# Three parts of W2 move behind transposed rows in the transfer queue

## The chip, the cores and the metric

The kernel runs on 1 core of one Trainium2 chip. The core has five engines with instruction streams of their own: TensorE (PE in the profile; its weight loads are PEld), VectorE (DVE), ScalarE (ACT), GpSimd (POOL) and SyncE (SP), which here issues every transfer. The metric is device time in microseconds (us), the median of several runs. Lower is better.

## The reference, cut to what matters

Two layers, each an attention block and an MLP with residuals, over 2048 rows of width 512. The same weights serve both layers.

```python
def _A_ref(x, wqkv, wo):                 # H = 32 heads of 16, window W = 256
    q, k, v = ...                        # from x @ wqkv
    scores = jnp.einsum("bhqd,bhkd->bhqk", q, k) * (Dh ** -0.5)
    mask = (idx[:, None] - idx[None, :] >= 0) & (idx[:, None] - idx[None, :] < W)
    p = _softmax(jnp.where(mask[None, None], scores, -1e9), axis=-1)
    return (...einsum("bhqk,bhkd->bhqd", p, v)...) @ wo

def _B_ref(x, w1, b1, w2, b2):           # F = 1792
    h = _gelu(jnp.einsum("bsd,df->bsf", x, w1) + b1)
    return jnp.einsum("bsf,fd->bsd", h, w2) + b2

x = A_x
x = x + _A_ref(_layernorm(x), A_wqkv, A_wo)
x = x + _B_ref(_layernorm(x), B_w1, B_b1, B_w2, B_b2)
x = x + _A_ref(_layernorm(x), A_wqkv, A_wo)
x = x + _B_ref(_layernorm(x), B_w1, B_b1, B_w2, B_b2)
```

## The kernel before

The 2048 rows are 16 tiles of 128 rows. Both layers run through one stream of 32 tile visits, numbered 0 to 31, in 16 blocks of two tiles. For a block, `lnq` and `kv` normalise the rows, bring them into transposed form (`xnTA`), and make Q, K and V from them; `attention` makes scores by pieces (L733), exponentials on ACT (L740), masks on DVE or POOL (L761), the product with V (PV, L783), and its normalisation; `outproj` adds the result to X (L832). Then the rows are normalised again and transposed into `xnTB` for the MLP. The MLP works in jobs; job 0 is tiles 0 and 1, job 1 tiles 2 and 3. It multiplies by W1 in 14 chunks of 128 columns, applies GELU (some after a bias addition on DVE, L855; the others on ACT directly, L863), and then for each tile sums the 14 chunks times W2 into one bank (L632, `gT` and `W2_sb`; W1 and W2 share the name W_sb in the profile), and adds the result to X (L875).

A row is transposed by DMA: DVE writes the normalised row to a buffer `xn` (L606), and SP issues a transposing DMA from it (L611). V needs a second copy with its halves exchanged, `Vs`, which two DMAs for each tile make (L681). Weights come in by pieces, W2 in four loads (L563): chunks 0 to 3 and 4 to 7 of 512 KB each, 8 to 10 and 11 to 13 of 384 KB each.

All steps of the kernel are nodes of a plan. The order is written out by hand in the list `_ORDER`: each engine carries out its own nodes in the order of this list, so the transfers, all on SP, go out in that order too. Before a node, its engine waits for the data it reads, for the readers of what it overwrites, and, for a DMA, for the eighth DMA before it, since eight semaphores are used in turn. An SP node that waits holds up every transfer behind it. The numbers in the list that matter here:

| node | transfer | waits for |
|---|---|---|
| 50, 51, 52, 53 | W2 chunks 0-3, 4-7, 8-10, 11-13 | nothing but the eighth DMA before |
| 242, 244 | rows of tiles 0 and 1 into `xnTB`, for job 0 | `xn` from DVE |
| 526, 528 | rows of tiles 8 and 9 into `xnTA`, for block 4 | `xn` from DVE |
| 185, 186; 192, 193 | copies of V of tiles 4; 5 | V of the tile |
| 357, 358; 364, 365 | copies of V of tiles 6; 7 | V of the tile |
| 646, 648 | rows of tiles 10 and 11 into `xnTA` | `xn` from DVE |

SP's order around the edit is: V copy of tile 4 (node 185), W2 chunks 4-7, 8-10, 0-3, rows of tiles 0 and 1, V copies of tiles 5, 6, 5, rows of tiles 9 and 8, W2 chunks 11-13, V copies of tiles 4 and 7, rows of tiles 11 and 10.

Of the kernel before, what the change touches and what calls it, by code (L numbers as in the profile page):

```python
# [19 lines left out]
class _Sched:  # L20
# [154 lines left out]
    208, 170, 213, 171, 172, 43, 330, 214, 370, 206, 173, 209, 148, 371, 174, 175, 210, 149, 160, 161, 162, 372, 331,  # L175
    176, 520, 163, 215, 177, 521, 374, 164, 373, 220, 44, 211, 376, 142, 165, 221, 178, 375, 45, 166, 167, 168, 180,
    522, 169, 222, 379, 223, 181, 380, 182, 230, 523, 224, 183, 524, 231, 381, 225, 179, 226, 369, 232, 233, 184, 227,
    384, 234, 378, 185, 228, 385, 332, 229, 333, 51, 383, 342, 187, 386, 52, 334, 235, 377, 343, 335, 50, 237, 344,
    337, 394, 388, 345, 396, 382, 338, 188, 238, 236, 387, 189, 239, 190, 395, 346, 339, 240, 389, 336, 191, 398, 243,
    641, 347, 400, 348, 349, 241, 340, 350, 390, 399, 242, 352, 359, 527, 244, 402, 391, 341, 392, 351, 353, 192, 403,  # L180
    354, 306, 355, 360, 356, 361, 404, 407, 639, 357, 362, 409, 363, 193, 248, 405, 249, 262, 528, 250, 263, 408, 412,
    264, 401, 252, 393, 253, 414, 245, 246, 254, 290, 255, 247, 256, 413, 427, 257, 563, 525, 410, 259, 565, 526, 260,
    278, 261, 279, 275, 564, 640, 416, 276, 411, 428, 53, 415, 272, 422, 287, 186, 397, 281, 282, 284, 365, 288, 285,
    277, 273, 423, 406, 280, 539, 289, 540, 566, 529, 251, 530, 541, 274, 531, 542, 283, 532, 543, 307, 265, 266, 267,
    258, 269, 270, 286, 308, 533, 309, 268, 310, 311, 271, 291, 312, 313, 417, 292, 418, 293, 314, 294, 315, 419, 567,
# [761 lines left out]
```

## Time and profile before

| | |
|---|---|
| median of 3 runs | 456.76 us (456.69 to 457.06) |
| profiled execution, time | 457.15 us |
| its span, first to last instruction | 455.3 us |
| PE busy | 420.6 us (92%) |
| ACT busy | 385.0 us (85%) |
| DVE busy | 352.7 us (77%) |
| POOL busy | 193.4 us (42%) |
| transfers, the queue of all DMAs from SP | 22.17 MB, 21.0% of 16 engines |
| mean granted TensorE clock | 0.996 |

Times of single instructions are microseconds from the start of the span. The busy share of an engine is an average over the span; what an edit is worth is read from the chain that ended last, which follows the work back from the last instruction, at each step to what released it. For a DMA, SP's own duration is only the issuing; the time to landing is counted from the start of the issue to the last of its sixteen completion signals.

### The profile page before, as it was taken

Reading aid. Unit: us, or ns where it says so; the run is one execution under the profiler, and the core shown is the slowest. Engines: PE = TensorE matmul, PEld = TensorE weight load, DVE = VectorE, ACT = ScalarE, POOL = GpSimd, SP = SyncE. Lnnn points to the kernel's source line nnn. Section 1 sums busy time; section 2 is a strip of 40 time slices with the busy share of each in tenths; the row PEclk is TensorE's granted clock in tenths of the full one; section 3 lists DMA queues with packets and bytes.
Section 4 is the critical chain, followed back from the end, with each engine's and each line's share of the span. In section 5 each row is a group of like instructions: output and inputs, shape, how many; then the busy total and the mean of one; then the engine's idle time right before and its main releaser. Section 6 shows DMA issues by size and latency. Waiting matters only on the chain.

```text
span 455.3 us, 16821 instructions
## 1 busy us (share of the span) xinstructions
PE 420.6 (92%) x7506; PEld 230.2 (51%) x7579; DVE 352.7 (77%) x655; ACT 385.0 (85%) x456; POOL 193.4 (42%) x217
## 2 busy tenths in 40 slices
PE   8998999985779997899999999999999999999997
PEld 4564646543344553445455454555554454444673
DVE  5999689886775778894799867977897598756862
ACT  2997968987889899789998998999888989899633
POOL 4164634237331247632472754274243443526130
PEclk9999999999899999999999999999999999999999
DMA  8695311201400211310012021010232003002110
GB/s 243 186 218 166 77 33 24 44 10 18 86 15 1 25 23 41 76 26 1 14 35 58 1 56 37 10 42 3 62 50 62 1 4 79 14 1 67 60 48 24
DMA packets 47972, 23.25 MB, mean 51 GB/s; under 512 B 33180, under 2 KB 47900, under 8 KB 47900
## 3 DMA queue, kind: packets, MB, share of 16 engines
q1 hardware_dynamic: 47900, 22.17, 21.0%
q8 instruction: 60, 0.98, 0.9%
q14 instruction: 12, 0.10, 0.1%
HBM read 8.00 MB, written 2.10 MB: 22 GB/s over the span
## 4 chain that ended last, share of the span: by engine, by line
PE 69%; DVE 15%; ACT 12%; issue 3%; DMA 2%; POOL 0%; SPq 0%
PE ps L632 52%; ACT E L740 11%; PE ps L733 8%; PE ps L783 7%; DVE KT L666 2%; DVE E L761 2%; DVE OD L792 2%; DVE xn L606 2%; PE ps L525 1%; DVE stat L584 1%; DMA xnTB<-xn 1%; DVE OT L806 1%; DVE X L832 1%; DMA xnTA<-xn 1%; DVE X L875 1%
## 5 line engine op out<-in xcount | busy, mean ns | idle before, releaser
L740 ACT ACTIVATE E<-ps 128x1024 bf16<-128x1024 f32 x300 | 283.1, 1041 | 42.4 <-PE ps L733 41.7
L761 POOL TENSOR_TENSOR E<-E,mask 128x512 bf16<-128x512 bf16 (+2 forms) x97 | 104.2, 1089 | 88.1 <-ACT E L740 88.0
L632 PE MATMUL ps<-xnTB,W_sb 128*128 128x512 bf16 (+1 forms) x542 | 110.2, 335 | 4.2 <-issue 1.6
L632 PE MATMUL ps<-W_sb,gT 128*128 128x512 bf16 x415 | 110.1, 380 | 3.3 <-issue 2.2
L761 DVE TENSOR_TENSOR E<-E,mask 128x512 bf16<-128x512 bf16 (+2 forms) x139 | 70.1, 529 | 10.3 <-ACT E L740 10.1
L632 PE MATMUL ps<-xnTA,Wqkv_sb 128*128 128x256 bf16 x512 | 74.6, 273 | 2.1 <-ACT E L740 0.7
L632 PEld LDWEIGHTS ps<-xnTB,W_sb 128*128 128x128 bf16 x560 | 50.6, 97 | 44.7 <-issue 4.1
L733 PE MATMUL ps<-QT,KT 32*128 32x128 bf16 (+3 forms) x1920 | 60.4, 232 | 10.9 <-ACT E L740 2.9
L632 PEld LDWEIGHTS ps<-W_sb,gT 128*128 128x128 bf16 x448 | 39.6, 98 | 43.2 <-issue 3.6
L733 PEld LDWEIGHTS ps<-QT,KT 32*128 32x128 bf16 x1920 | 28.6, 93 | 62.5 <-ACT E L740 36.9
L632 PEld LDWEIGHTS ps<-xnTA,Wqkv_sb 128*128 128x128 bf16 x512 | 46.9, 98 | 25.3 <-issue 3.9
L792 DVE STREAM_TRANSPOSE OD<-ps 128x1024 f32<-128x1024 f32 x32 | 39.8, 1244 | 21.5 <-PE ps L783 21.2
L863 ACT ACTIVATE gT<-ps,b1T 128x512 bf16<-128x512 f32 (+1 forms) x80 | 43.6, 609 | 10.3 <-PE ps L632 9.9
L871 POOL TENSOR_TENSOR Xb<-X,b2all 128x512 f32<-128x512 bf16 x32 | 38.5, 1209 | 24.8 <-DVE X L875 24.8
L783 PE MATMUL ps<-E,Va 64*17 64x128 bf16 (+3 forms) x1920 | 44.0, 230 | 4.1 <-ACT E L740 1.8
L666 DVE TENSOR_TENSOR KT<-ps,parmask 128x1024 bf16<-128x1024 f32 x32 | 38.8, 1212 | 11.1 <-PE ps L632 10.8
L783 PE MATMUL ps<-E,Vs 64*17 64x128 bf16 (+3 forms) x1920 | 44.6, 230 | 0.0
L783 PEld LDWEIGHTS ps<-E,Va 64*17 64x17 bf16 x1920 | 37.4, 84 | 13.9 <-issue 8.8
L584 DVE BATCH_NORM_STATS2 stat<-X 128x6 f32<-128x512 bf16 x64 | 42.7, 677 | 1.8 <-DMA X<-in_A_x_dram 1.7
L855 DVE TENSOR_SCALAR gT<-ps,b1T 128x512 bf16<-128x512 f32 (+1 forms) x60 | 36.5, 629 | 7.0 <-PE ps L632 6.4
L800 POOL TENSOR_TENSOR Nb<-OD,Rc 128x512 bf16<-128x512 f32 x19 | 20.2, 1061 | 49.9 <-DVE Rc L796 39.6
L632 PE MATMUL ps<-Wo_sb,OT 128*128 128x512 bf16 x120 | 37.2, 388 | 3.4 <-DVE OT L806 2.5
(50 smaller groups left out, 363.0 us busy)
## 6 DMA issues: line engine op xcount, KB each, us to landing
Vs<-Va SPq DMA_DIRECT2D x64, 68.0 KB, 2.1
W_sb<-in_B_w_dram SPq DMA_DIRECT2D x4, 512.0 KB, 5.5
out_dram<-X SPq DMA_DIRECT2D x16, 128.0 KB, 1.9
X<-in_A_x_dram SPq DMA_DIRECT2D x3, 512.0 KB, 7.3
Wqkv_sb<-in_A_wqkv_dram SPq DMA_DIRECT2D x4, 256.0 KB, 5.3
W_sb<-in_B_w_dram SPq DMA_DIRECT2D x1, 768.0 KB, 6.5
W_sb<-in_B_w_dram SPq DMA_DIRECT2D x2, 384.0 KB, 4.8
Wqkv_sb<-in_A_wqkv_dram SPq DMA_DIRECT2D x1, 512.0 KB, 7.1
```

The lines of the kernel that those rows point to most:

```text
L584: add("dve", lambda e, B, t=t, k6=k6: e.bn_stats(stat6[:, k6, :], X[:, t, :]), reads=["X%d" % t], writes=["st%d" % k6], key="bs%d" % (k + j))
L632: r = e.matmul(ps[:, B[g][0], cols], lhsT, rhs, start=st, stop=sp)
L666: add("dve", lambda e, B, g=g, i=i: e.tensor_tensor(out=KT[:, kb, 2 * i : 2 * i + 2].rearrange("p c m a q -> p a (c m) q"), in0=ps[:, B[g] ...
L733: x = e.matmul(ps[:, bk[r], o : o + n], KT[rows, kb, c, m].rearrange("p a q -> p (a q)"), QT[rows, c, q : q + n], start=True, stop=True)
L740: add("act", lambda e, B, g_=g_, gi=gi: e.activation(E[:, 2 * gi : 2 * gi + 2, e0 : e0 + 512], ps[:, B[g_][0] : B[g_][0] + 2, :], AF.Exp, ...
L761: fn = lambda e, B: e.tensor_tensor(out=Ew, in0=Ew, in1=Mw, op=ALU.mult)
L783: x = e.matmul(ps[32 * r : 32 * r + VW, B[g][par], c % 2 * 2 * P + lo : c % 2 * 2 * P + hi], V[rows, (2 * b + m // 2) % VR, c * HC + 2 * r ...
L792: add("dve", lambda e, B: e.transpose(OD[:, s].rearrange("p a c q -> p (a c q)"), ps[:, B[g][0] : B[g][0] + 2, :]), reads=["ps:" + g], wri ...
L800: return e.tensor_tensor(out=Nb[:, s, :].rearrange("p (k a d) -> p a k d", a=2, d=Dh), in0=sums[:, :, :, 0:Dh], in1=rc[:, :, :, None].to_b ...
L855: add("dve", lambda e, B, g=g, fc=fc: e.tensor_scalar(out=gT[:, fc, c0 : c0 + M], in0=ps[:, B[g][0], 0:M], scalar1=b1T[:, fc : fc + 1], sc ...
L863: add("act", lambda e, B, g=g, fc=fc: e.activation(gT[:, fc, c0 : c0 + M], ps[:, B[g][0], 0:M], AF.Gelu_apprx_tanh, bias=b1T[:, fc : fc + ...
L871: add("pool", lambda e, B, t=t, xs=xs: e.tensor_tensor(out=Xb[:, xs, :], in0=X[:, t, :], in1=b2all[:], op=ALU.add), reads=["X%d" % t, "b2a ...
```

## The change

Only `_ORDER` differs. Nodes 51, 52 and 50 leave their places after the V copy of tile 4. Nodes 50 and 51 (W2 chunks 0 to 7) stand after node 244 (tile 1's row into `xnTB`); node 52 (chunks 8 to 10) stands after node 526 (tile 8's row into `xnTA`), ahead of node 53. SP's order becomes: V copy of tile 4, rows of tiles 0 and 1, W2 chunks 0-3 and 4-7, V copies of tiles 5, 6, 5, rows of tiles 9 and 8, W2 chunks 8-10, 11-13, V copies of tiles 4 and 7, rows of tiles 11 and 10. No other engine's order changes, and no instruction is added or taken away. Cut to the lines where nodes enter or leave:

```diff
-    384, 234, 378, 185, 228, 385, 332, 229, 333, 51, 383, 342, 187, 386, 52, 334, 235, 377, 343, 335, 50, 237, 344,
...
-    641, 347, 400, 348, 349, 241, 340, 350, 390, 399, 242, 352, 359, 527, 244, 402, 391, 341, 392, 351, 353, 192, 403,
...
-    264, 401, 252, 393, 253, 414, 245, 246, 254, 290, 255, 247, 256, 413, 427, 257, 563, 525, 410, 259, 565, 526, 260,
+    384, 234, 378, 185, 228, 385, 332, 229, 333, 383, 342, 187, 386, 334, 235, 377, 343, 335, 237, 344, 337, 394, 388,
...
+    348, 349, 241, 340, 350, 390, 399, 242, 352, 359, 527, 244, 50, 51, 402, 391, 341, 392, 351, 353, 192, 403, 354,
...
+    401, 252, 393, 253, 414, 245, 246, 254, 290, 255, 247, 256, 413, 427, 257, 563, 525, 410, 259, 565, 526, 52, 260,
```

## The prediction

> **What bounds the kernel now.** I read the page first. TensorE (PE) is busy for 92% of the span, and the chain that ended last lies mostly on it, so a transfer counts only where PE, or an engine that PE waits for, stands still for it.
>
> ```profile
> span 455.3 us, 16821 instructions
> ...
> PE 69%; DVE 15%; ACT 12%; issue 3%; DMA 2%; POOL 0%; SPq 0%
> ```
>
> DMA has 2% of the chain, 9 us, and the transfer queue itself (SPq) nothing. So the question is whether the moved loads touch that 2%, or get into the way of a transfer that has slack today. All that moves lies between 33 and 56 us. Next I read SP's own timeline there (start, duration, line, operation).
>
> ```profile
> 32.56 0.46 SPq L681 DMA_DIRECT2D Vs<-Va  x1
> 33.07 2.47 SPq L563 DMA_DIRECT2D W_sb<-in_B_w_dram  x3
> 39.42 2.51 SPq L611 DMA_TRANSPOSE xnTB<-xn  x2
> 41.98 2.86 SPq L681 DMA_DIRECT2D Vs<-Va  x3
> 44.88 5.25 SPq L611 DMA_TRANSPOSE xnTA<-xn  x2
> 50.18 0.59 SPq L563 DMA_DIRECT2D W_sb<-in_B_w_dram  x1
> 50.82 1.13 SPq L681 DMA_DIRECT2D Vs<-Va  x2
> ```
>
> The three W2 loads are issued from 33.07 to 35.54; then SP issues nothing until 39.42, the transpose of tile 0. What it waits for stands in SP's waits of 32 to 52 us (total, times, longest):
>
> ```profile
> SPq L127 <- DVE xn L606: 5.9, 2, 3.8
> SPq L127 <- ACT Va L575: 3.3, 1, 3.3
> SPq L127 <- DVE Va L573: 1.1, 1, 1.1
> ```
>
> The 3.8 us are the gap before tile 0's transpose: the normalised row `xn` was not ready, and it went out 0.1 us after DVE had written it (39.34). The other 2.1 us of that line are the gap before tile 8's transpose (46.77 to 48.94). The 1.1 us are the gap between tile 5's and tile 6's V copies (42.56 to 43.73). Then the chain of waits (start, duration, what):
>
> ```profile
> 39.03 0.32 DVE xn L606
> 39.35 1.16 DVE OD L792
> ...
> 44.30 0.61 PE ps L632 x4
> ...
> 47.62 1.26 DVE xn L606
> ...
> 48.95 3.09 DMA xnTA<-xn
> ...
> 52.08 1.92 PE ps L632 x16
> ```
>
> From 36 to 42 us DVE carries it (the windows view has DVE busy 6.00 of 6.00 us). At 44.30 PE begins the MLP of tiles 0 and 1. At 48.95 tile 8's transpose is on the chain: 3.09 us to landing, and PE stands still 0.40 us for it. That is the only transfer on the chain near the edit.
>
> **Part 1: three loads leave the place ahead of tile 0.** SP gives back 2.47 us of issuing inside a stretch in which it idles 3.9 us (35.54 to 39.42) for DVE. Value 0. The rings were nearly clear as well: the last of the three, the part for chunks 0 to 3, landed at 40.28, yet the two transposes issued at 39.42 and 40.66 landed after 2.48 and 2.51 us, and the median of all 30 into xnTB is 2.5 us. Both had landed by 43.18, while PE asks for them at 44.30, released there by ACT freeing a bank and not by a DMA. So no gain on either side of the queue. [...]
>
> **Part 2: chunks 0 to 7 behind tile 1's transpose.** Two issues of 0.54 to 0.59 us (1.25 at worst, the third one of 33.07) now stand at 41.98, ahead of tile 5's first V copy, tile 6's, tile 5's second, tile 9's transpose and tile 8's. Cost on SP: 2 x 0.6 = 1.2 us, at worst 2.5. The 1.17 us gap before tile 6's copy takes the first, the 2.17 us gap before tile 8's transpose the next: 3.3 us of cover against 1.2 to 2.5. So tile 8's transpose still goes out at 48.94, released by DVE. If that cover were gone, every us would be on the chain.
>
> In the rings: 1 MB starts at about 43.4, by the 1.2 to 1.4 us between issue and first packet of the later load. While the three loads ran alone they moved 0.37 MB per us (36 to 38 us), so 1 MB takes 2.8 us, up to 46.3, and lands by about 47.5. The bounds come from issue to landing of the same loads: 4.3 us (the one at 50.18) to 6.0 us (the third of the three): 46.3 to 48.7. The copies of tiles 5 and 6 then land at up to 49 instead of 44 to 47.5; their first reader is the PV product of block 2 at 70.7. Tile 9's row lands at 48 to 49.5 instead of 47.93; its reader waits for tile 8's row, 52.03, anyway. All 0.
>
> The one tight place is tile 1's row, which now has 1 MB right behind it. Two rows followed directly by weights show what that does: tile 6's (ahead of W1) took 3.32 us and tile 8's (ahead of the last W2 part) 3.09 us, against 2.5 without. So tile 1's row lands 0.6 to 0.8 us later, at 43.8 to 44.0; PE asks at 44.30. Cost 0, with 0.3 us left. The slowest row near here (tile 3's, 4.35 us) gives the upper bound: landing at 45.0, +0.7 us.
>
> PE needs chunk 0 when it first loads from gT with W2, at 53.7 us, and chunk 4 at 55.35: 5 us after the worst landing. Cost 0.
>
> **Part 3: chunks 8 to 10 behind tile 8's transpose.** This 384 KB load takes the place, at 50.18, of the equal one for chunks 11 to 13, which follows at 50.8. Tile 8's row therefore keeps the same kind of neighbour, and its 3.09 us; a gain or a loss on the chain is excluded as far as size goes. Chunks 8 to 10 land at 54.5 (the present load's 4.3 us); counting the chunks in PE's timeline they are read at 58.55. Chunks 11 to 13 land at 55.5 to 56.8 (4.7 to 6.0 us) and are read at 60.08. Spare: 4.0 and at least 3.3 us. The copies of tiles 4 and 7 go out 0.6 us later and are read after 70 us; SP's next issue waits for DVE until 61.75. Cost 0.
>
> [...]
>
> **Sum.** 0 - 0 + 0, with -0.4 (PE's wait for tile 8's row) and +0.7 us (tile 1's row) as ends. The profiled execution is 457.15 us (455.3 of span and 1.85 around it), 0.4 above the median of the runs, 456.76. I carry the difference, 0, over to the median: 456.8 us.
>
> **The rivals.** *Slower: full rings hold SP up, and tile 8's row goes out late.* By today's durations, with the two loads added, SP has issued tile 9's row by 46.9 (41.98, the two loads 1.2, the copies 0.6, 0.5 and 0.6, tile 9's 1.9). For the rival: with several 512 KB loads in the rings an issue took 1.6 us (at 5.35 and 7.95) instead of 0.6, and the longest transpose issue is 2.57 us (at 85.37) instead of 1.9. If the second load and two of the copies take 1.6 and tile 9's row 2.6, that is 3.7 us more: tile 8's row goes out at 50.6 instead of 48.94, and the 1.7 us are on the chain at once, 458.5 us; with tile 1's row late as well (+0.7), 459.2. It decides from the point where SP is still issuing tile 9's row at 48.94. Against it: two loads are in flight, not four or more, and tile 7's transpose, issued 2.3 us after a W1 load into busy rings, took SP 1.25 us only. Late data alone does not do it: even if the second load needed the 7.8 us that one took with several ahead of it, it would land at 50.4, and the rows behind it before 52. Chance 0.22.
>
> *Faster: another meeting of DVE and POOL.* Tile 8's `xn` takes 1.33 us where its equals take 0.40, with a mask multiply on POOL beside it; so does one mask on DVE (1.50 against 0.54). A small shift of the start of the MLP could part such a pair, 0.9 us for each: 455.9, or 455.4 together with the 0.4 us before 52.08. Against it: POOL's operations there follow one another without a gap, so a shift by 0.3 us parts nothing. Chance 0.10.
>
> *It does not free what it says it frees.* The rows of tiles 0 and 1 never queued behind W2. That is no rival but my forecast, and the time is unchanged: chance 0.68.
>
> **How the numbers follow.** About 0.2% (0.9 us) is what a measurement of this kernel can tell from no change. My forecast's own range is 456.3 to 457.5, from the ends -0.4 and +0.7. The range for 8 in 10 reaches up to 458.2, into the slower rival, whose price begins at nothing and goes past 458.5 (about 0.12 is left out there), and down to 456.0, just above the faster one's 455.9 (0.06 left out).
>
> **What would show it.** Right: tile 0's transpose is still issued at 39.4, SP idle before it from 33 us on; tile 1's row lands at 43.8 to 44.0, PE's first MLP matmul at 44.3; tile 8's transpose issued at 48.9, PE at 52.1; no PE wait on a W2 load; the chain after 56 us the same piece by piece. Wrong: tile 0's transpose before 39, a PE wait for xnTB at 44 or a longer one than 0.40 us for xnTA at 52, or a PE wait on W_sb between 53 and 61.

## The result, and the profile after

The changed kernel takes 456.23 us (median of 22 runs), the kernel before 457.13 us beside it (22 runs). The ratio is 0.9976, with an interval of 0.9969 to 0.9984: faster by 0.24%, or 0.9 to 1.1 us. The prediction had said no change that can be told. The profiled execution took 456.32 us, its span is 454.6 us against 455.3.

The chain's shares and SP's own timeline of the kernel after (start, duration, line, operation):

```profile
PE 74%; DVE 14%; ACT 9%; DMA 2%; issue 1%; POOL 0%; SPq 0%
```

```profile
32.73 0.46 SPq L681 DMA_DIRECT2D Vs<-Va  x1
39.59 2.51 SPq L611 DMA_TRANSPOSE xnTB<-xn  x2
42.16 1.13 SPq L563 DMA_DIRECT2D W_sb<-in_B_w_dram  x2
43.33 2.36 SPq L681 DMA_DIRECT2D Vs<-Va  x3
45.73 3.61 SPq L611 DMA_TRANSPOSE xnTA<-xn  x2
49.38 1.11 SPq L563 DMA_DIRECT2D W_sb<-in_B_w_dram  x2
50.54 1.14 SPq L681 DMA_DIRECT2D Vs<-Va  x2
```

The queue did what was forecast. Tile 0's transpose still goes out when DVE has written the row, at 39.59, after 6.3 us of waiting instead of 3.8. No row gained by having no W2 ahead (the two into `xnTB` landed after 2.4 and 2.5 us, before after 2.48 and 2.51). And yet PE's first weight load for the MLP starts 0.9 us earlier (43.38 instead of 44.27), and `issue` fell from 3% of the chain to 1%. The place is 2.6 us before that, where PE takes up the scores of block 1's eighth piece. PE's weight loads from 39.4 to 42 us, first of the kernel before, then after (in brackets: idle time before, and what ended it):

```profile
39.63 0.11 PEld L632 LDWEIGHTS ps<-Wqkv_sb,xnTA 128*128 128x128 bf16 x2 [0.21 <-ACT E L740]
41.74 0.23 PEld L733 LDWEIGHTS ps<-QT,KT 32*128 32x128 bf16 x12 [1.99 <-issue]
```

```profile
39.76 0.11 PEld L632 LDWEIGHTS ps<-Wqkv_sb,xnTA 128*128 128x128 bf16 x2 [0.21 <-ACT E L740]
40.79 0.23 PEld L733 LDWEIGHTS ps<-QT,KT 32*128 32x128 bf16 x12 [0.92 <-ACT E L740]
```

Before, PE stood 1.99 us for `issue`: for nothing that the profile shows. After, it stands 0.92 us, and ACT's exponential ends the wait. The chain of before had put the same wait down to DVE's `QT`, which ended at 41.61; after the change `QT` ends at 41.78 and the scores have begun at 40.79, so they never needed it.

What PE lacked, by the runs below, was its own program. Queue 8, kind "instruction", carries 60 packets of 16 KB, and the trace of the kernel after holds 15320 PE instructions (7579 matmuls, as many weight loads, and 162 of its sequencer), 255 for each packet. The profile counts its packets, like those of SP's transfers, on the core's 16 DMA engines (1.0% of them over the span, SP's queue 21.0%; both shares below are shares of them); "the rings" stands for these engines' queues of work. The queues from 36.8 to 38.9 us (packets, MB, share of the 16 engines), before and after:

```profile
q1 hardware_dynamic: 780, 0.77, 109.2%
```

```profile
q8 instruction: 1, 0.02, 2.6%
```

Before, W2 fills the rings there, and the program's packet begins only at 38.96. After, the rings hold nothing else and it begins at 37.97. The runs below show steps of 256 instructions: PE's 1.99 us of `issue` end at instruction 1217 of the trace, and the other stops that moved with the program lie at 29, 37, 50 and 54 times 256 from there. Counted through the whole trace of the kernel after, the packets of queue 8 pair in order with such blocks of 256. In 48 of 58 pairs the packet begins after PE has entered the block just before, and the median is 0.9 us after; the ten that begin earlier were not looked into.

### The profile page after: what moved, and what is told of

The parts are those of the page before. It is cut to its first block, busy times and chain, and to the rows that moved or that the text cites. A ratio compares the mean times of both kernels' runs of the same rounds, so it can differ in the third digit from the quotient of the medians.

```text
span 454.6 us, 16894 instructions
## 1 busy us (share of the span) xinstructions
PE 430.2 (95%) x7579; PEld 230.4 (51%) x7579; DVE 353.7 (78%) x655; ACT 385.4 (85%) x456; POOL 192.9 (42%) x217
## 4 chain that ended last, share of the span: by engine, by line
PE 74%; DVE 14%; ACT 9%; DMA 2%; issue 1%; POOL 0%; SPq 0%
PE ps L632 56%; ACT E L740 8%; PE ps L783 8%; PE ps L733 8%; DVE KT L666 2%; DVE E L761 2%; DVE OD L792 2%; DMA xnTA<-xn 2%; DVE stat L584 2%; PE ps L525 1%; DVE xn L606 1%; DVE Va L573 1%; DVE OT L806 1%; DVE X L832 1%; DVE X L875 1%
## 5 line engine op out<-in xcount | busy, mean ns | idle before, releaser
L632 PE MATMUL ps<-W_sb,gT 128*128 128x512 bf16 x448 | 118.0, 380 | 0.0
L632 PE MATMUL ps<-xnTB,W_sb 128*128 128x512 bf16 (+1 forms) x560 | 114.5, 337 | 1.2 <-ACT E L740 0.8
L632 PEld LDWEIGHTS ps<-W_sb,gT 128*128 128x128 bf16 x448 | 39.6, 98 | 43.2 <-issue 3.4
L632 PE MATMUL ps<-Wo_sb,OT 128*128 128x512 bf16 x128 | 39.4, 386 | 1.7 <-DVE OT L806 1.6
```

Source lines behind the costliest of these rows:

```text
L632: r = e.matmul(ps[:, B[g][0], cols], lhsT, rhs, start=st, stop=sp)
```

## The experiments

The theory, "fetch", is my assumption, which the runs below test: PE can't enter a block of 256 instructions before its 16 KB have come; they are asked for when the block before is entered (read here from the start of its first instruction; the asking itself stands in no trace), they share the DMA rings with the weights, and W2 in the rings made this one late (it began 2.14 us after that entry, after the change 0.97). Rivals: "rows" (the gain is the transposed rows' clear way), "meeting" (DVE and POOL lie differently at tile 8's `xn`), and a real wait for `QT`.

**One part alone.** First only chunks 0 to 7, then only chunks 8 to 10:

```diff
 e1_part1: ... 333, 51, 383, ... 50, 237   ->   333, 383, ... 237     (52 stays at its early place)
           ... 527, 244, 402               ->   527, 244, 50, 51, 402
 e2_part2: ... 386, 52, 334                ->   386, 334              (51 and 50 stay at their early places)
           ... 565, 526, 260               ->   565, 526, 52, 260
```

> Only chunks 0 to 7 of W2 (1 MB) stand behind tile 1's row; chunks 8 to 10 (384 KB) keep their early place at 33 us. Theory 'fetch': PE runs out of instructions after 39.7 us because the block of 16 KB of its program that is on queue 8 at 38.96 was held up by W2 in the rings; 384 KB alone have left the rings by about 36.5, before that block is asked for (36.8). So its packet comes at about 38.0, PE's gap is 0.9 to 1.0 us instead of 2.0, and the time is that of the whole change, ratio 0.997 to 0.999. Rival 'meeting': the gain comes from DVE and POOL lying differently at tile 8's xn (0.91 instead of 1.33 us); then the gap at 39.7 is beside the point, and this kernel gains only if xn of tile 8 takes under 1.0 us whatever PE's gap is. Rival 'rows': the gain comes from transposed rows clear of W2, tile 0 and 1 here; then their landing must come earlier after issue than 2.5 us.

> Only chunks 8 to 10 (384 KB) stand behind tile 8's row; chunks 4 to 7 and 0 to 3 (1 MB) keep their early places. Theory 'fetch': 1 MB is in the rings from about 35 to 38 us, so the block asked for at 36.8 still waits, to 38 or 39; PE's gap 1.0 to 2.0 us, ratio 0.998 to 1.000, nearer to 1 than the first part alone. Rival 'rows' (tile 8's row clear of the last W2 part): as large a gain as the whole change, by an earlier landing of tile 8's row counted from its issue (3.09 us before). Rival 'meeting': as the xn of tile 8 falls out.

Measured: 455.49 us, ratio 0.9975 (0.9961 to 0.9989) to the kernel before, run beside it, as all ratios below, and 455.22 us, 0.9964 (0.995 to 0.9977). Either part brings the whole gain. In the first the packet begins 0.84 us after the block before was entered (36.46), in the second 1.30 us (37.02), against 2.14 us in the kernel before. The gap is 0.92 and 0.94 us, and in both ACT ends it. So the second expectation was wrong by its size: when the block before was entered, 0.4 MB of the 1 MB was left to move, and the packet came 0.46 us later than in the first part; that is still early enough, since ACT's exponential (over at 40.63) holds the scores as long. This also tells why the two parts don't add up. "Rows" falls: in the first part alone tile 1's row took the same 2.5 us, in the second tile 8's took 3.1 us as before.

**The old loads back, the new ones kept.**

```diff
 for i in order:
     S_.op(nd["eng"], ...)
+    for p in early.get(i, ()):          # early = {185: (1, 2, 0)}: W2 parts, once more at their old place
+        nd = PL.nodes[50 + p]
+        S_.op("sp", ..., writes=phys(nd["writes"]), dma=True)
```

> The changed order, but the three W2 loads are also made once at their old places (the same bytes twice, 1.4 MB more). Theory 'fetch': the old loads are back in the rings from 35 to 39 us, so the block's packet is back at about 39 and PE's gap at 39.7 back at 2.0 us, although no row stands behind a load that was not there before the change and the late loads are as in the change; the time goes back to the kernel before, ratio 0.999 to 1.001. Rival 'rows' and rival 'the late places themselves bring the gain': the late loads are unchanged, so the time stays at 0.997 to 0.999.

Measured: 457.56 us, ratio 1.0018 (1.0005 to 1.0031). The packet begins at 39.19, 2.31 us after its block's predecessor was entered. PE's weight loads, and DMA from 36 to 38 us (the last two columns: share of the 16 engines, GB/s), first of this kernel, then, for comparison, of the first part alone:

```profile
41.85 0.23 PEld L733 LDWEIGHTS ps<-QT,KT 32*128 32x128 bf16 x12 [2.10 <-issue]
```

```profile
36.00:38.00 2.00, 1.94 (x133) 1.47 (x130) 2.00 (x3) 1.76 (x3) 1.14 (x2) 1.00 1.10 379
```

```profile
36.00:38.00 2.00, 1.94 (x139) 1.40 (x136) 2.00 (x5) 1.34 (x2) 0.80 (x2) 1.00 0.03 8
```

With W2 moving 379 GB/s there, the stop of 2.1 us is back, although PE reads nothing of those bytes before they are loaded again; with 8 GB/s it isn't. The time is back as well. That it lies 0.2% above the kernel before, beyond the 0.999 to 1.001 expected, was not looked into; up to block 4's first projection this kernel and that of before take the same time, as the table below shows.

**Is it the block, or a wait of the scores?** The kernel before, then the changed one, with 36 more instructions in PE's warm-up (on a zero tile that nothing reads) and nothing else:

```diff
-            add("pe", lambda e, B, bk=h % 8: e.matmul(ps[:, bk, :], gT[:, 0, 0:P], gT[:, 0, :], start=True, stop=True),
...
+            def warm(e, B, bk=h % 8):
+                for c in range(2):
+                    r = e.matmul(ps[:, bk, c * 256 : c * 256 + 256], gT[:, 0, 0:P], gT[:, 0, 0:256], start=True, stop=True)
+                return r
...
```

> The kernel before, with each of the 18 warm-up matmuls of 512 columns made as two of 256: 36 more PE instructions in the first 8 us, no other work, order or wait changed. Theory 'fetch': the ends of the 256-instruction blocks come 36 instructions earlier in the real work. The gap of 2.0 us at sc1_7 (the scores at 41.7) leaves that place and shows up 36 instructions earlier, in the K and Q projections near 38.5, as 2 to 3.5 us; the 1.8 us gap at 112 moves or goes; new gaps of 0.5 to 2.5 us open at blocks that PE runs through in under 3.7 us (by the trace near 200, 243, 263, 307, 394, 426), and the time grows by 3 to 12 us (ratio 1.007 to 1.026). Rival 'the wait at 41.7 is one for DVE's QT, as the chain has it': the gap stays at sc1_7, 2.0 us, and the time stays within 0.3%.

> The changed order together with the split warm-up of e4_split_before (36 more PE instructions at the start). There PE ran out 36 instructions earlier, at 37.61, stood until 41.63, 2.5 us after the block's packet (39.11, 2.86 us after the block before it was entered), and the granted clock was halved from 39.6 to 46.5. Theory 'fetch': with W2 out of the rings at 36 to 39 us the packet comes 0.9 to 1.3 us after the block is entered, near 37.4, PE goes on near 39.8 to 40.2, the gap is 2.2 to 2.6 us and short enough to leave the clock at full rate there; the edit is then worth 2.5 to 5 us in this pair, 462 to 465 us against 467.2. Rival 'the edit brings a fixed 0.9 to 1.3 us by where W2 and the rows stand': 466 us.

Measured: 467.24 us, ratio 1.0225 (1.0185 to 1.0265), and 463.52 us, 1.0145 (1.0106 to 1.0184). PE's long stops of the first, then of the second:

```profile
41.64 0.13 PEld L737 LDWEIGHTS ps<-QT,KT 32*128 32x128 bf16 x6 [3.93 <-issue]
...
317.78 0.10 PEld L737 LDWEIGHTS ps<-QT,KT 32*128 32x128 bf16 x3 [1.77 <-issue]
```

```profile
39.68 0.11 PEld L737 LDWEIGHTS ps<-QT,KT 32*128 32x128 bf16 x6 [1.69 <-issue]
...
314.88 0.10 PEld L737 LDWEIGHTS ps<-QT,KT 32*128 32x128 bf16 x3 [1.76 <-issue]
```

The stop leaves the eighth piece of the scores and stands inside the seventh (x6: six of that piece's eight loads), 36 instructions earlier in the real work and again at count 1217; I had expected it a little later, in the projections. In the first kernel new stops begin at 252, 316 and 438 us, before the instructions with the counts 8642, 10690 and 15041 (counted in the second, whose trace is complete): 29, 37 and 54 times 256 further on, to within one instruction. The second has the first two of them, and one at 14018, 50 times 256. No data dependency has that period. The wait for `QT` is refuted, and so is my expectation that the 1.8 us gap at 112 would move: it stays at its instruction, and is a wait for data.

W2 in the rings costs more here, since PE gets to the end of the block sooner (at 37.7 us instead of 39.75): it stood 3.93 us with W2 there and 1.69 us without (2.2 to 2.6 expected), and the edit is worth 3.7 us instead of 0.9, by medians of 4 runs each, which spread over 5 to 6 us. Part of that is the clock: the six score matmuls behind the long stop took 0.61 us together, behind the short one 0.39. The first of these two kernels, from 39.6 to 46.4 us (PEclk is the third column from the end):

```profile
39.60:46.40 6.80, 4.54 (x31) 2.35 (x33) 2.84 (x5) 2.40 (x3) 2.17 (x2) 0.50 0.26 51
```

The granted clock fell to 0.50 at 39.6, 1.9 us into the long stop (37.7 to 41.6), and stayed there for 6.8 us; with the short stop, 1.69 us, it stayed at 1.00. The 2.2 to 2.6 us that I had expected to be short enough for this did not occur. What brings the clock down was not shown: in the kernel before, the stop of 1.99 us left it at 1.00 (38 to 46 us), yet it was 0.50 from 115.9 to 119.3 us, and in the 3.4 us ahead of that PE was busy for 0.55 and never stood longer than 1.75 at once.

**W2 earlier instead of later, and the whole change again.**

```diff
 e6_early: ... 45, 166   ->   45, 51, 52, 50, 166     (node 45: last part of W1)
```

> The kernel before, with the three W2 loads one place earlier in the queue, ahead of tile 4's first V copy: issued from 29.3 instead of 33.1 us, so W2 follows W1 without a pause and has left the rings by about 38 instead of 39.2. All rows and copies but that one stay as they were before the change. Theory 'fetch': the block asked for at 36.8 goes out near 38 to 38.5 instead of 38.96, PE's gap at 39.7 falls to 1.0 to 1.5 us, ratio 0.997 to 0.999. If the block before it (asked for at 27.8) is held up beyond 34 us, a gap opens at 36.8 instead and the time rises, 1.000 to 1.003. Rival 'W2 must stand behind the rows': no gain, 0.999 to 1.001, and the gap at 39.7 stays 2.0.

> The second part alone once more, beside the whole change on one chip. Theory 'fetch': its gap at 39.7 is the same 0.95 us as the whole change's, since there ACT's exponential ends last and not the block; so the two agree within 0.1%. If moving 1 MB behind tile 1's row has a price of its own (tile 9's row landed at 50.3 instead of 47.9, tile 8's at 51.35), the second part alone is faster by 0.1 to 0.2%.

> The whole change once more, to stand beside the second part alone: ratio 0.997 to 0.9985 to the kernel before.

Measured: early 455.63 us, ratio 0.9985 (0.9969 to 1.0001), inconclusive as a time; second part 455.39, 0.9972 (0.9958 to 0.9986); whole change 455.37, 0.9975 (0.9964 to 0.9985). The early kernel's profile is clearer: 0.4 MB was left when the block was entered, the packet came 0.88 us later, and the gap was 0.93 us, ended by ACT. W2 need not stand behind any row for that. The second part alone and the whole change can't be told apart by time.

The eight traces at these places, each counted from the sixth piece of block 1's scores (34.8 us before), so that differences in the first loads drop out; "W2 left" is what the queue of SP's transfers still moved after the block was entered, up to the end of the early loads:

| kernel | W2 left | packet after entering | scores at | tile 8's `xn` takes | block 4's first K at |
|---|---|---|---|---|---|
| before | 0.9 MB | 2.14 us | +6.91 | 1.33 us | +17.24 |
| reload | 0.8 MB | 2.31 | +6.97 | 1.33 | +17.25 |
| part 2 | 0.4 MB | 1.30 | +5.84 | 0.92 | +16.28 |
| part 2 again | 0.4 MB | 1.05 | +5.83 | 0.92 | +16.28 |
| part 1 | 0 | 0.84 | +5.79 | 0.92 | +16.39 |
| early | 0.4 MB | 0.88 | +5.83 | 0.92 | +16.29 |
| whole change | 0 | 0.97 | +5.79 | 0.91 | +16.40 |
| whole change again | 0 | 0.85 | +5.79 | 0.92 | +16.42 |

**Fewer instructions.** The changed order without the last three, then the last six, of the 18 warm-up matmuls:

```diff
+            if nd["key"] in ["warm%d" % h for h in range(NWARM - 3, NWARM)]:    # e10: NWARM - 6
+                continue
```

> The changed order with the last 3 of the 18 warm-up matmuls left out (work on a zero tile that nothing reads): 6 PE instructions fewer, so each 256-instruction block ends 6 instructions later in the real work. Theory 'fetch': no block gets shorter than about 3.2 us (0.9 us to the packet, 2.3 after it), the block of 395 us, 3.35 us long with a gap of 0.46 at its end, lasts longer, and no gap opens elsewhere; -0.2 to -0.6 us against the changed kernel, ratio 0.996 to 0.998. If the number of instructions is without effect: 0.9975 as the changed kernel.

> As e9_warm15 with the last 6 warm-up matmuls left out: 12 instructions fewer. By the spacing of the blocks in the trace after the change, blocks of 3.1 to 3.4 us come up near 68, 220 and 338 us, right at the 3.2 us that a block needs: gaps of 0 to 0.3 us, ratio 0.996 to 0.999. If the shorter warm-up leaves the clock at half rate past 8 us: 1.000 to 1.004.

Measured: 456.39 us, ratio 0.999 (0.9977 to 1.0002), and 456.18 us, 0.9989 (0.998 to 0.9998): no better than the changed order. The stop at the end of the block of 395 us went as expected, but one of 0.69 and 0.71 us opened in the PV product near 71, where a block without its stop takes PE 3.0 to 3.4 us and the packet came 1.65 and some 1.3 us after the block before was entered. I had taken 0.9 us for the packet there. Why it came later is open: SP had just issued a transposed row (68.57 and 68.88), but queue 1 moved nothing from 66 us until after the packet had begun (68.96 and 69.26). So the two kernels show again that the count decides where the stops lie, and no version that beats the changed one.

## Why the prediction was wrong

**The step that failed is the first: "Value 0", and with it "So no gain on either side of the queue".** I priced W2's leaving by what shares SP's queue with it: SP's time and the rows' landing. Both were right. I did not ask who else used the rings between 35 and 39 us: PE's own program, on queue 8. Its packet came 1.0 us earlier after the change, and the scores, counted as in the table, 1.12 us. That 456.23 us lies inside the range given for 8 in 10 (456.0 to 458.2) is luck: the range reached down there for another mechanism.

**The reading behind it** was the chain of waits. From 36 to 42 us I let DVE carry it, by DVE's 6.00 of 6.00 us, and so did not look at PE's 1.99 us of `issue` in that stretch. A releaser that ended 0.1 to 0.2 us before the start had the credit, and a word that looks like "nothing to see" had the cause.

**Parts 2 and 3 held, with errors of size.** Tile 1's row landed after 2.5 us at 43.3, not 43.8 to 44.0: weights right behind it did not slow it. W2's chunks landed at 47.1 and 49.2 (I had up to 48.7), tile 9's row at 50.3 (up to 49.5), tile 8's at 51.35 after 3.21 us (3.09), chunks 8 to 13 at 53.1 and 54.6, before their reading. No PE wait on W2 appeared. The 1 MB does cost 0.1 us at block 4's first K, by the table: +16.39 to 16.42 with it behind tile 1's row, +16.28 and 16.29 without.

**The size of the gain.** The chain of the kernel after, from 37 to 56 us:

```profile
41.24 0.54 DVE QT L573
41.78 1.12 DVE KT L666
42.90 0.60 DVE Va L573
43.50 0.60 DVE stat L584
44.10 0.59 DVE Va L573
44.69 0.78 DVE gT L855 x2
...
47.24 0.84 DVE xn L606
...
48.15 3.21 DMA xnTA<-xn
...
51.41 4.52 PE ps L632 x32
```

Once PE is early, DVE is what ends last up to 47 us, and of PE's lead only 0.38 us is left when tile 8's `xn` begins (47.16 instead of 47.54). That `xn` then takes 0.91 instead of 1.33 us: 0.42 more. Tile 8's row lands 0.12 us slower. Together 0.68 us, and block 4's first K starts 0.67 us earlier (51.41 instead of 52.08), which is the 0.7 us by which the span is shorter. So the faster rival, "another meeting of DVE and POOL", did have a part in it, but as a consequence: in all eight traces `xn` takes 1.33 us where PE stood 2 us, and 0.91 or 0.92 where it didn't. That POOL's mask beside it is the reason was not tried by itself. The slower rival did not occur: SP had issued tile 9's row by 47.0 and waited for DVE before tile 8's.

## What to carry to other kernels

When a transfer is moved, ask who else uses the rings at both its places: the instruction queue was one of the users here (60 packets of 16 KB for PE's 15320 instructions), and the one that decided (1.1 us for one packet behind 0.9 MB of weights). Read `issue` on the weight loads as a question, and see whether the stop stays with an instruction or with a count: a few more instructions ahead of it answer that in one run, and where stops stay with the count, the length of the program ahead of a dense stretch is itself a tuning knob (36 idle instructions cost 2.25% here). A releaser in the chain is shown only when the work starts at its heels in a second kernel too.

## What the runs showed of the hardware

In the kernels that kept W2 out of the way, the block that begins at count 1217 had its packet 0.8 to 1.0 us after the block before was entered; in the kernel after, this packet took 0.88 us. Where PE stood for a block, it went on 2.4 to 2.8 us after the packet's start (in the kernel before from 38.96 to 41.74, with 15 and 12 warm-up matmuls from 68.96 to 71.39 and from 69.26 to 71.74). So, as an estimate from the lower of these numbers (0.8 + 2.4), 256 instructions that PE runs through in less than some 3.2 us end in a stop, if the packet is as prompt. Dense stretches got there by themselves: in the changed kernel with the longer warm-up, the blocks at 247 to 250 and 312 to 315 us took 3.3 us each, of which 0.82 and 1.76 us were the stops at their ends. Of the 59 crossings of the kernel before all but three are without a stop (the three: 0.4, 0.6 and 1.99 us of `issue`), and the one with 0.9 MB of weights ahead of its packet, the longest, cost 1.1 us.
